# GpSimd relieved of sums and lo parts after attention, and a new order of the attention phase's pieces

## The chip, the cores and the metric

The kernel runs on one core of a Trainium2 chip. The core has five engines that run side by side, each through its own queue in order: TensorE (PE, matrix products into PSUM), VectorE (DVE), ScalarE (ACT), GpSimd (POOL) and SyncE (SP, which here issues nearly all DMAs). The metric is the device time of one execution in microseconds (us), the median of some runs.

## The reference, cut to what matters

```
q, k, v: (batch 2, 8 heads, 768, 64) float32
k_sum = max over blocks of 32 keys;  v_sum = mean over the same blocks        (24 summaries a head)
scores = concat(windowed q.kT / 8 with |i-j| < 16,  q.k_sumT / 8 + log 32);  a = softmax(scores)
x  = a @ concat(v, v_sum)              -> (1536 tokens, 512)
x  = relu(x @ w_in)**2 @ w_out         first layer, d_ff 2048
y  = gelu_sigmoid(x @ w_in2) @ w_out2  second layer, d_ff 2048    (float32; the kernel's weights arrive as 64-bit words)
```

## The kernel before, in words

**Precision.** A product of float32 operands is made of three single-pass products: each operand is split into a hi part (rounded) and a lo part (the rest), and PE adds hi·hi, hi·lo and lo·hi. `parts` (from L906) makes the two: the hi part by ACT (L913) or DVE (L914), the lo part, a subtraction of two operands in SBUF, by DVE or GpSimd (L918). `add` (from L892) makes sums and differences of two SBUF tiles on DVE or GpSimd (L902). Weights arrive as 512 KB `raw` tiles (L871 for w_in, L875 for w_out); ACT scales the upper words (L880), DVE puts the number together (L884, L887), and `parts` splits it. Some are saved to DRAM for a second use (L853) and fetched again (L857).

**Work.** The attention phase handles 12 tiles of 128 tokens. For a unit of 256 tokens, q and k are loaded and turned by PE: with `packed` 0 or 1 by four transposes for each half (L557), with `packed` 2 by eight products of 64 columns for each half (L561), whose load moves rows of 512 bytes in two DMAs of 256 KB (L411) instead of rows of 256 bytes (L418, `packed` 0). The first 768 keys come by another way (L432, L439, turned at L603). The summaries of v come from PE (L533, L507) out of three v loads of 512 KB each. `scores` (PE L692, DVE L707), `softmax` (ACT L722, DVE and GpSimd L726, L736, L729) and `tail` (PE L759 and L771, ACT L325) follow for each tile; a tail writes the tile's columns of `xh` and `xl`, the operands of the first layer. The first layer for tokens 0 to 511 runs among these pieces, block f of d_ff after block: `step` (PE L953 into `h`) and `finish` (PE L1008 into `acc`). Its first four blocks run in halves of 256 tokens (matmuls of 256 columns).

After attention the rest is matrix work. `layer` runs the second layer on tokens 0 to 511 (L953, L1010). `twice` runs each layer for the other 1024 tokens with fewer products: seven instead of eight for a 2x2 block matrix (L1395), once for w_in and, for 6 or 8 pairs of blocks, once more for w_out (`second`, L1300 in the first layer, L1302 in the second). The price is sums and differences of tiles (L902, `add`) and sums of a PSUM bank with an SBUF tile (L1309). In the second layer's `twice`, each of the eight pairs of blocks goes round one loop: products into three banks, sums out of them, the activation (ACT L1162), the differences t1 and t2 and their split into `gh` and `gl` (L902, L913, L918), and a `second` with them, for which PE waits; at the same time the next pair's weights are combined (four differences on half tiles of 128x256, twice: w_in for the next pair, w_out for this one).

**What sets the order.** `ORDER` lists the attention phase's pieces: `K`/`B` loads of k, `T` their turning, `q`, `k` loads of a unit (second number: the packing), `V` the v summaries, `w,f,z` a weight block (z 0: w_in, 1: w_out), `g` or `h` scores and softmax, `t` a tail, `s,f,half` and `S,f` a step. A planner goes through this list and then through the code after it. It puts each operation at the first gap of its engine at which its inputs are ready by its own table of costs, and at the end everything is emitted in the order of planned starts. So the place of a piece in `ORDER` says who asks first for an engine, not where the piece ends up, and each engine runs its list in order, waiting where the plan was wrong. The queue of SP is such a list too: a load whose buffer isn't free holds up all loads behind it.

For operations that two engines can do, `soonest` takes the one that ends first by the plan. GpSimd's choices carry `port=True`: the planner lets GpSimd and DVE's operations of that kind take turns on one shared line. After the attention phase, GpSimd's planned times are stretched by 1.25 (`SLACK`), and DVE gets a handicap (`LEAN`). `ALONE` is read in `soonest`, after attention alone:

```
if eng == "POOL" and port and self.alone:
    continue
```

In the planned gaps of PE up to the first use of bank acc3, short matmuls of the identity (`warm`, L1728) are put that compute nothing.

Of the kernel before, what the change touches and what calls it, by code (L numbers as in the profile page):

```python
# [22 lines left out]
CHAIN = "b2cp4p56"  # L23
EARLY = 1
AHEAD = (0, 1, 2)
ALONE = False
SLACK = 0.05, 1.25
LEAN = 1.5, 0.25
MIX = (2, 3, 4, 5)
# [4 lines left out]


ORDER = """
    m,1 sel K,1 m,2 B,1 m,0 w,0,0 K,0 B,0 T,0 T,1 q,0,2 T,2 T,3 tq,0 q,1,1 g,1,0 g,1,1 tq,1 selw V,0 V,1 V,2
    v,0 h,2,0 v,1 g,0,1 q,2,2 q,3,0 k,3,0 ps,0 t,1 h,3,0 h,2,1 g,0,0 tq,2 v,2 t,0 h,3,1 w,3,0 t,2 v,3 h,5,0
    tq,3 w,0,1 s,0,0 t,3 w,3,1 h,4,0 k,5,0 s,3,0 w,2,0 s,0,1 w,2,1 s,2,0 s,2,1 k,4,1 q,4,1 tk,3 v,4 w,1,0
    h,5,1 h,4,1 v,5 v,6 w,1,1 tk,4 tk,5 s,3,1 t,4 pk,3 w,6,0 t,5 h,6,0 w,7,0 s,1,0 sv,1 w,6,1 s,1,1 pk,4  # L40
    w,7,1 h,7,0 S,7 tq,4 w,4,0 w,4,1 h,7,1 S,6 w,11,0 w,11,1 pk,5 h,9,0 q,5,0 S,4 w,9,0 h,6,1 v,7 S,11 v,8
    ps,1 w,8,0 t,7 h,9,1 w,9,1 tq,5 w,10,0 w,10,1 S,9 v,9 w,15,0 t,6 w,8,1 t,9 S,8 w,5,0 S,10 w,12,0 h,10,0
    w,5,1 w,14,0 h,10,1 S,5 v,10 h,11,0 w,12,1 w,14,1 S,12 w,13,0 h,11,1 h,8,0 S,14 t,10 v,11 w,15,1 S,15
    h,8,1 t,11 w,13,1 S,13 t,8
"""


# [222 lines left out]
def kernel(  # L270
# [1428 lines left out]
    plan.lean = LEAN  # L1699
    plan.alone = ALONE  # L1700
    plan.slack = SLACK
# [60 lines left out]
```

## Time and profile before

| | us |
|---|---|
| median of 3 runs (lowest, highest) | 573.71 (573.65, 575.44) |
| the profiled execution, its own time | 576.52 |
| its span, first to last instruction | 574.8 |
| PE busy (share of the span) | 560.5 (98%) |
| DVE busy | 495.4 (86%) |
| ACT busy | 409.2 (71%) |
| GpSimd busy | 87.7 (15%) |

PE's busy time is a union of modelled, pipelined matmuls: that it is near 100% says that PE nearly always had a matmul under way, and a matmul of 512 columns starts every 0.23 us in a stretch without waits. The chain that ended last runs through PE for 79% of the span, through DVE for 10% and through DMAs for 6%.

### The profile page before, as it was taken

How to read it: one execution, taken by the hardware profiler on the slowest of the kernel's cores; microseconds unless marked ns; L12 is line 12 of the kernel's file. 1: busy time of each engine (PE TensorE's matmuls, PEld its weight loads, DVE VectorE, ACT ScalarE, POOL GpSimd, SP SyncE). 2: the span in 40 equal slices, each digit the busy share in tenths (PEclk: the TensorE clock that was granted, in tenths of full speed). 3: DMA queues.
4: the chain of work that ended last, by engine and by line, in shares of the span. 5: the costliest groups of instructions: out<-in, count | busy, mean ns of one | idle time of the engine just before them, and what ended most of it. 6: DMA issues, size and time to landing. Idle time of an engine off the chain costs nothing.

```text
span 574.8 us, 10960 instructions
## 1 busy us (share of the span) xinstructions
PE 560.5 (98%) x3766; PEld 476.8 (83%) x3766; DVE 495.4 (86%) x1072; ACT 409.2 (71%) x892; POOL 87.7 (15%) x153
## 2 busy tenths in 40 slices
PE   9899999999999999999999999999999999999997
PEld 8678888877878887888887888888778888899997
DVE  4788888989789999988998998989988888889983
ACT  5998889878886678787788856666456555687660
POOL 6323321012100000000020101001131233200200
PEclk9999999999999999999999999999999999999999
DMA  9999998897678765544668758574355554587653
GB/s 267 235 245 244 291 279 261 258 291 221 192 230 263 243 210 178 169 148 164 202 203 259 217 155 267 164 237 148 135 177 178 159 177 147 180 268 240 203 154 110
DMA packets 106711, 120.25 MB, mean 209 GB/s; under 512 B 32832, under 2 KB 74560, under 8 KB 106656
## 3 DMA queue, kind: packets, MB, share of 16 engines
q1 hardware_dynamic: 106464, 119.17, 68.4%
q8 instruction: 29, 0.48, 0.4%
q0 software_dynamic: 192, 0.39, 0.2%
q14 instruction: 26, 0.21, 0.1%
HBM read 86.64 MB, written 32.51 MB: 207 GB/s over the span
## 4 chain that ended last, share of the span: by engine, by line
PE 79%; DVE 10%; DMA 6%; ACT 2%; issue 1%; SPq 1%; POOL 0%; POOLq 0%; DVEq 0%
PE acc L1395 11%; PE m L1395 9%; PE acc L1302 8%; PE h L953 8%; PE acc L1008 7%; PE acc L1300 7%; PE m L1300 5%; PE m L1302 4%; PE acc L953 4%; PE m L1010 3%; PE acc L1010 2%; DMA raw<-in_moe_w_in_dram 2%; PE h L1302 2%; PE h L1300 2%; PE m L771 2%; PE m L953 1%
## 5 line engine op out<-in xcount | busy, mean ns | idle before, releaser
L918 DVE TENSOR_TENSOR w<-xw,w 128x512 fp32r<-128x512 f32 (+1 forms) x138 | 83.7, 621 | 4.5 <-ACT w L913 3.5
L913 ACT CAST w<-xw 128x512 fp32r<-128x512 f32 (+1 forms) x132 | 70.5, 552 | 21.8 <-DVE xw L887 14.9
L953 PE MATMUL h<-xh,w 128*128 128x512 f32 (+1 forms) x184 | 55.7, 365 | 1.3 <-DVE w L918 0.7
L880 ACT ACTIVATE raw<-raw 128x512 f32<-128x512 f32 x72 | 48.1, 680 | 8.4 <-DMA raw<-in_moe_w_out_dram 6.2
L1395 PE MATMUL m<-top,w 128*128 128x512 f32 x210 | 53.5, 392 | 0.6 <-ACT w L325 0.6
L887 DVE SCALAR_TENSOR_TENSOR xw<-raw,xw 128x512 uint32<-128x512 uint32 x68 | 46.7, 688 | 3.9 <-ACT raw L880 1.7
L1395 PEld LDWEIGHTS m<-top,w 128*128 128x128 f32 x210 | 38.6, 188 | 8.9 <-ACT w L325 1.4
L1395 PE MATMUL acc<-top,w 128*128 128x512 f32 x174 | 44.5, 391 | 0.0
L1008 PE MATMUL acc<-gh,w 128*128 128x512 f32 (+1 forms) x160 | 42.2, 350 | 0.1
L1395 PE MATMUL acc<-xh,w 128*128 128x512 f32 x124 | 41.8, 389 | 0.0
L953 PEld LDWEIGHTS h<-xh,w 128*128 128x128 f32 x184 | 33.1, 188 | 8.0 <-DVE w L918 1.0
L884 DVE TENSOR_SCALAR xw<-raw 128x512 uint32<-128x512 uint32 x68 | 29.1, 429 | 11.6 <-DMA raw<-in_moe_w_in_dram 9.3
L1395 PEld LDWEIGHTS acc<-top,w 128*128 128x128 f32 x174 | 32.2, 188 | 7.3 <-ACT w L325 0.4
L722 ACT ACTIVATE sm<-sm,st 128x120 f32<-128x120 f32 x96 | 36.6, 385 | 0.2
L913 ACT CAST top<-gs 128x512 fp32r<-128x512 f32 x40 | 24.7, 619 | 13.6 <-DVE gs L902 5.1
L953 PE MATMUL h<-xl,w 128*128 128x512 f32 (+1 forms) x92 | 32.8, 356 | 0.3 <-DVE xl L784 0.3
L1008 PEld LDWEIGHTS acc<-gh,w 128*128 128x128 f32 x160 | 27.8, 189 | 4.3 <-issue 0.5
L918 DVE TENSOR_TENSOR top<-gs,top 128x512 fp32r<-128x512 f32 x38 | 27.0, 713 | 3.0 <-ACT top L913 2.5
L1302 PE MATMUL acc<-w,gh 128*128 128x256 f32 x136 | 28.2, 283 | 0.0
L1008 PE MATMUL acc<-gl,w 128*128 128x512 f32 (+1 forms) x80 | 27.9, 349 | 0.0
L1395 PEld LDWEIGHTS acc<-xh,w 128*128 128x128 f32 x124 | 23.3, 188 | 4.9
L918 DVE TENSOR_TENSOR w<-w,w 128x256 fp32r<-128x256 f32 (+1 forms) x48 | 24.8, 522 | 1.6 <-ACT w L913 1.4
(301 smaller groups left out, 1532.1 us busy)
## 6 DMA issues: line engine op xcount, KB each, us to landing
raw<-in_moe_w_in_dram SPq DMA_DIRECT2D x36, 512.0 KB, 4.9
raw<-in_moe_w_out_dram SPq DMA_DIRECT2D x36, 512.0 KB, 4.5
w<-xw SPq DMA_DIRECT2D x52, 256.0 KB, 2.5
xw<-w SPq DMA_DIRECT2D x29, 256.0 KB, 2.8
w<-w SPq DMA_DIRECT2D x23, 256.0 KB, 2.8
g<-r SPq DMA_DIRECT2D x16, 256.0 KB, 2.1
r<-g SPq DMA_DIRECT2D x16, 256.0 KB, 3.2
vw<-in_v_dram SPq DMA_DIRECT2D x20, 192.0 KB, 6.2
```

What stands on the lines that cost most here:

```text
L722: nc.scalar.activation(out=s.t[:, h, :], in_=s.t[:, h, :], func=AF.Exp, bias=st.t[:, 0, h:h + 1], scale=-1.0, accum_out=st.t[:, 1, h:h + 1])
L880: nc.scalar.activation(out=top, in_=top, func=AF.Prelu, scale=-(2.0 ** -80), alpha=-(2.0 ** -32))
L884: op("DVE", 0.36, lambda: nc.vector.tensor_scalar(out=x.t, in0=raw.t[:, :, 0], scalar1=29, scalar2=None, op0=ALU.logical_shift_right), rea ...
L887: op("DVE", 0.64, lambda: nc.vector.scalar_tensor_tensor(out=x.t, in0=raw.t[:, :, 1], scalar=3, in1=x.t, op0=ALU.logical_shift_left, op1=A ...
L913: plan.soonest([("ACT", 0.09 + 0.44 * fr, False, lambda: nc.scalar.copy(out=hi.t[:, hc], in_=src())), ("DVE", 0.05 + 0.4 * fr, True, lambd ...
L918: eng.tensor_tensor(out=lo.t[:, lc], in0=src(), in1=hi.t[:, hc].bitcast(F32), op=ALU.subtract)
L953: nc.tensor.matmul(hp.t[:, cols], lhsT=w.t[:, kc * P:(kc + 1) * P], rhs=x.t[:, kc, cols], start=(kc == 0 and n == 0), stop=(kc == KC - 1 a ...
L1008: nc.tensor.matmul(a.t[:, cols], lhsT=w.t[:, j * P:(j + 1) * P], rhs=g.t[:, cols], **st)
L1010: nc.tensor.matmul(a.t, lhsT=g.t[:, j * P:(j + 1) * P], rhs=w.t, **st)
L1300: nc.tensor.matmul(b.t, lhsT=w.t[:, x + j * P:x + j * P + P], rhs=g.t, **st)
L1302: nc.tensor.matmul(b.t[:, (j % 2) * CH:(j % 2) * CH + CH], lhsT=g.t[:, j * P:j * P + P], rhs=w.t[:, x:x + CH], **st)
L1395: nc.tensor.matmul(bank.t, lhsT=a, rhs=rhs(b, kh), start=(begin and k == 0 and n == 0), stop=(k == 1 and n == 2), skip_group_check=True)
```

## The change

Two things are changed, both numbers and no code. `ALONE` becomes True: in the code after the attention phase, GpSimd is no longer offered sums (`add`, `whole`), lo parts (`parts`, and the `gl` of `step`). What reads PSUM was never offered to it. And `ORDER` is another list: the same 16 weight blocks, 12 tiles and 6 units, in another order, with other packings of some loads (q1, k3, k4 now 2, before 1, 0, 1; q2 now 0, before 2; q3 and k5 now 1, before 0), and with other weight blocks first.

```
-ALONE = False
+ALONE = True
 ...
-    m,1 sel K,1 m,2 B,1 m,0 w,0,0 K,0 B,0 T,0 T,1 q,0,2 T,2 T,3 tq,0 q,1,1 g,1,0 g,1,1 tq,1 selw V,0 V,1 V,2
 ...
+    B,0 selw w,3,0 m,2 m,0 K,0 T,0 T,1 K,1 B,1 T,3 q,0,2 T,2 tq,0 w,1,0 w,0,0 g,1,0 q,1,2 sel tq,1 m,1 g,0,1
 ...
```

**SP's queue at the start of the program.** `kin` holds k and later v, `qin` q, `raw` a weight block, `vw` the windows of v. Before:

```order
L432 DMA kin_103<-in_k_dram 128x4x256
L439 DMA kin_108<-in_k_dram 128x4x128
L871 DMA raw_116<-in_moe_w_in_dram 128x4x256
L432 DMA kin_137<-in_k_dram 128x4x256
L439 DMA kin_108<-in_k_dram 128x4x128
L411 DMA qin_182<-in_q_dram 128x4x128 x2
L411 DMA qin_212<-in_q_dram 128x8x128
L432 DMA kin_244<-in_v_dram 128x4x256
L432 DMA kin_266<-in_v_dram 128x4x256
L439 DMA kin_290<-in_v_dram 128x8x128
```

and in the changed kernel:

```order
L439 DMA kin_87<-in_k_dram 128x4x128
L871 DMA raw_97<-in_moe_w_in_dram 128x4x256
L432 DMA kin_119<-in_k_dram 128x4x256
L432 DMA kin_147<-in_k_dram 128x4x256
L439 DMA kin_87<-in_k_dram 128x4x128
L411 DMA qin_165<-in_q_dram 128x4x128 x2
L871 DMA raw_208<-in_moe_w_in_dram 128x4x256
L871 DMA raw_231<-in_moe_w_in_dram 128x4x256
L411 DMA qin_255<-in_q_dram 128x4x128 x2
L432 DMA kin_288<-in_v_dram 128x4x256
L432 DMA kin_310<-in_v_dram 128x4x256
L439 DMA kin_333<-in_v_dram 128x8x128
```

Three weight blocks (blocks 3, 1 and 0) now stand ahead of the three v loads, where one stood.

**DVE in the second layer's `twice`, one turn of the loop** (t1 and t2 are the first two differences of 128x512, `xw` and `part` combined weights of w_in and w_out). Before:

```order
L902 TENSOR_TENSOR xw_5651<-w_5607 128x256
L902 TENSOR_TENSOR xw_5653<-w_5574,w_5607 128x256
L902 TENSOR_TENSOR r_5662<-gs_2710,w_5546 128x512
L902 TENSOR_TENSOR r_5667<-gs_2771,r_5662 128x512
L902 TENSOR_TENSOR gs_2710<-gs_2771,gs_2710 128x512
L918 TENSOR_TENSOR gl_5683<-r_5662,gh_5669 128x512
L918 TENSOR_TENSOR gl_5687<-r_5667,gh_5675 128x512
L1309 TENSOR_TENSOR w_5692<-acc_5647,r_5655 128x512
L918 TENSOR_TENSOR w_5640<-w_5607,w_5640 128x256
```

and in the changed kernel:

```order
L902 TENSOR_TENSOR r_5679<-gs_2756,w_5565 128x512
L902 TENSOR_TENSOR r_5684<-gs_2817,r_5679 128x512
L902 TENSOR_TENSOR gs_2756<-gs_2817,gs_2756 128x512
L918 TENSOR_TENSOR gl_5700<-r_5679,gh_5686 128x512
L918 TENSOR_TENSOR gl_5704<-r_5684,gh_5692 128x512
L1309 TENSOR_TENSOR w_5709<-m_5666,r_5672 128x512
L902 TENSOR_TENSOR xw_5717<-w_5618 128x256
L902 TENSOR_TENSOR xw_5723<-w_5603,w_5618 128x256
L902 TENSOR_TENSOR xw_5717<-xw_5717,w_5603 128x256
L902 TENSOR_TENSOR xw_5723<-w_5603,xw_5717 128x256
```

The four differences of w_in, of which DVE did two ahead of t1 and GpSimd two beside t1 and t2, now all stand on DVE behind `gl`. The order of PE's instructions in this loop (36 of L1395, 12 of L1302, 6 of L1395, 12 of L1302) is the same in both.

## Rows read from the trace of the kernel before

**Rows 1.** Busy time in stretches: start:end, length, each engine's busy us (instructions), PEclk, DMA, GB/s.
```profile
0.00:25.00 25.00, 21.81 (x346) 18.94 (x348) 13.74 (x62) 16.64 (x53) 11.50 (x56) 1.00 0.98 255
25.00:50.00 25.00, 23.39 (x340) 20.90 (x336) 21.90 (x91) 22.22 (x79) 6.88 (x14) 1.00 1.09 252
50.00:75.00 25.00, 23.25 (x289) 21.08 (x287) 20.62 (x54) 22.03 (x65) 10.26 (x22) 1.00 1.02 259
...
275.00:300.00 25.00, 25.00 (x111) 20.58 (x110) 23.86 (x47) 19.89 (x37) 3.22 (x3) 1.00 0.61 196
...
163.00:575.00 412.00, 404.01 (x2080) 343.88 (x2078) 362.87 (x656) 273.84 (x510) 46.28 (x43) 1.00 0.60 192
```

**Rows 2.** What PE waited for, whole span: total us, times, longest.
```profile
PE m L1302 <- DVE gl L918: 3.4, 5, 1.2
PE m L533 <- DMA kin<-in_v_dram: 1.5, 2, 1.2
...
PE h L953 <- DVE w L918: 0.7, 1, 0.7
PE m L1395 <- ACT w L325: 0.6, 1, 0.6
```

**Rows 3.** Timeline of a turn with GpSimd beside DVE: start, duration, engine, instruction, [idle before].
```profile
444.95 0.69 DVE L1309 TENSOR_TENSOR gs<-m,r 128x512 f32<-128x512 f32 x1 [1.09 <-PE m L1395]
446.71 0.80 POOL L902 TENSOR_TENSOR xw<-xw,w 128x256 f32<-128x256 f32 x1 [4.79 <-DVE xw L902]
446.83 1.22 DVE L902 TENSOR_TENSOR r<-gs,w 128x512 f32<-128x512 f32 x1
...
448.61 1.19 POOL L902 TENSOR_TENSOR part<-xw 128x256 f32<-128x256 f32 x1
...
450.19 0.28 PE L1302 MATMUL m<-w,gh 128*128 128x256 f32 x1
450.27 1.28 DVE L918 TENSOR_TENSOR gl<-r,gh 128x512 fp32r<-128x512 f32 x2
451.00 0.39 PE L1302 MATMUL m<-w,gl 128*128 128x256 f32 x1 [0.54 <-DVE gl L918]
...
463.42 0.28 PE L1302 MATMUL m<-w,gh 128*128 128x256 f32 x1
```

**Rows 4.** Timeline of the turn before it, without GpSimd in these operations.
```profile
435.62 0.69 DVE L902 TENSOR_TENSOR gs<-gs,gs 128x512 f32<-128x512 f32 x1
436.23 1.29 DVE L918 TENSOR_TENSOR gl<-w,gh 128x512 fp32r<-128x512 f32 x2
...
437.75 0.28 PE L1302 MATMUL m<-w,gh 128*128 128x256 f32 x1
...
438.03 0.41 DVE L902 TENSOR_TENSOR xw<-xw,w 128x256 f32<-128x256 f32 x1
```

**Rows 5.** Groups by shape, DVE, from 163 us on: count | busy us, mean ns.
```profile
L902 DVE TENSOR_TENSOR gs<-gs,gs 128x512 f32<-128x512 f32 x30 | 23.7, 791 | 0.1
```

**Rows 6.** The chain that ended last, in the attention phase: start, us, what.
```profile
12.28 7.08 DMA kin<-in_v_dram
...
28.37 7.04 DMA raw<-in_moe_w_in_dram
...
54.38 7.01 DMA raw<-in_moe_w_out_dram
```

**Rows 7.** Timeline of PE in the attention phase.
```profile
11.61 1.92 PE L561 MATMUL m<-ident,qin 128*64 128x128 f32 x32
...
37.64 0.39 PE L953 MATMUL h<-xh,w 128*128 128x256 f32 x1 [0.55 <-ACT xh L325]
...
57.91 1.04 PE L557 MATMUL m<-ident,kin 128*128 128x128 f32 x8
58.70 0.36 PE L953 MATMUL h<-xh,w 128*128 128x256 f32 x1
```

**Rows 8.** PE's groups by line from 0 to 75 us: the matmuls that compute nothing.
```profile
L1728 PE MATMUL warm<-ident 128*128 128x128 f32 x34 | 6.8, 354 | 1.4 <-POOL ident masks.py:199 1.4
```

More of the change, by code (lines that the diff above doesn't have):

```diff
@@ L36 @@
 ORDER = """
-    m,1 sel K,1 m,2 B,1 m,0 w,0,0 K,0 B,0 T,0 T,1 q,0,2 T,2 T,3 tq,0 q,1,1 g,1,0 g,1,1 tq,1 selw V,0 V,1 V,2
[L38 to L44, printed above, removed]
+    B,0 selw w,3,0 m,2 m,0 K,0 T,0 T,1 K,1 B,1 T,3 q,0,2 T,2 tq,0 w,1,0 w,0,0 g,1,0 q,1,2 sel tq,1 m,1 g,0,1
+    g,1,1 V,0 V,1 V,2 v,0 g,0,0 v,1 v,2 ps,0 t,1 h,3,0 k,3,2 t,0 h,2,0 w,1,1 h,2,1 k,4,2 v,3 h,3,1 s,1,0
+    tk,3 t,3 w,0,1 q,2,0 tk,4 t,2 s,0,0 w,3,1 tq,2 w,2,0 h,4,0 w,2,1 s,3,0 k,5,1 s,0,1 s,3,1 s,2,0 q,3,1
+    s,2,1 q,5,0 s,1,1 tq,3 w,9,0 w,4,0 tk,5 h,5,0 pk,3 w,7,0 w,7,1 w,4,1 w,6,0 S,4 h,7,0 tq,5 S,7 v,4 pk,5
+    h,4,1 w,9,1 t,4 S,9 w,5,0 w,8,0 sv,1 h,6,0 v,5 pk,4 h,5,1 h,7,1 w,8,1 v,6 w,11,0 S,8 t,5 q,4,1 w,11,1
+    w,6,1 S,6 tq,4 S,11 h,9,0 w,5,1 w,12,0 S,5 w,10,0 ps,1 h,6,1 v,7 t,7 h,11,0 w,10,1 w,15,0 S,10 w,12,1
+    w,13,0 v,8 v,9 t,6 h,8,0 S,12 v,10 h,11,1 v,11 w,14,0 h,9,1 t,9 t,11 h,8,1 h,10,0 w,15,1 w,13,1 w,14,1
+    S,15 t,8 S,14 h,10,1 S,13 t,10
 """
```

## Prediction

> **What bounds the kernel now.** I read the busy time by stretches first, then what PE waited for, then the timeline of the stretches in which it waited, last the chain of waits. From 75 us on PE is full nearly everywhere: 25.00 of 25 us in a stretch such as 275 to 300 [rows 1]. So nothing that only shifts work on DVE, ACT or GpSimd there counts, unless PE waits for it. PE loses time in three places. At the start, in 75 us, it is idle for 3.19 + 1.61 + 1.75 = 6.55 us [rows 1], and 34 matmuls of 6.8 us compute nothing [rows 8]; part of that is the wait for the first load, which no order can take away. In the second layer's `twice` it waits five times, 3.4 us in all, for a lo part `gl` of DVE, and once 0.6 us for ACT just ahead of that loop [rows 2]. The rest is the end of the program. So the change has two halves that hardly touch: `ALONE` acts on the five waits, `ORDER` on the first 75 us.
>
> **ALONE: the five waits.** After 163 us GpSimd does 43 operations in 46.28 us [rows 1], 33 of them of 128x256 and 10 of 128x512. In a turn of the loop with GpSimd, its differences run from 446.71 to 449.80; beside them DVE's difference of 128x512 takes 1.22 us, the next ones as long, and `gl` is ready so late that PE, which came at 450.19, goes on at 451.00 [rows 3]. In the turn before, without GpSimd in this place, the same difference takes 0.69 us, the step from one such operation to the next is 0.61 us, and PE doesn't wait [rows 4]. In the changed order seven operations of 128x512 lead from the sum L1309 to the first `gl`: 7 x 0.61 = 4.3 us after 444.95 is 449.2, a microsecond before PE comes. GpSimd's differences now stand on DVE behind `gl`; their users come a third of a turn later. So the wait should go in all five turns. What it is worth: 3.4 us by the waits; by the turns, 463.42 - 450.19 = 13.23 us with a wait [rows 3] against 450.19 - 437.75 = 12.44 without [rows 3, 4], 0.8 us four times and about 1.5 for the first, longest one, 4.7 us. The low end is 1.5 us, if half of the waits come back as waits for the weights combined later. I take 3.8, nearest to the waits themselves with a part of the 0.6 us.
>
> **ALONE: what DVE gets for it.** By 0.41 us for 128x256 [rows 4] and 0.69 for 128x512 [rows 4], the 43 operations are 33 x 0.41 + 10 x 0.69 = 20.4 us at most, against 412 - 362.87 = 49 us in which DVE is free [rows 1]. It saves what the sharing costs now: at least 30 x (0.79 - 0.69) = 3 us, in the one group of differences that shows it best [rows 5], at most half of GpSimd's 46 us, 23. In the loop that matters it is 3 x 0.53 = 1.6 us saved [rows 3, 4] for three operations of 0.41 = 1.2 us added, so a turn gets no longer. In 275 to 300 us DVE is busy 23.86 of 25 us and takes over three operations, 0.41 + 0.41 + 0.69 = 1.5 us, for 3.22 us of GpSimd [rows 1]: with a third of that saved it stays just under 25. I cost this at nothing; its cover is the buffers between DVE and PE, and without cover a lag of 1 us or so could reach PE.
>
> The Trainium skill, GPSIMD Engine Reference, section Key points, says that GpSimd shares its SBUF interfaces with VectorE, which contends when VectorE's instruction has two SBUF inputs. By that rule the doubling seen in rows 3 goes with GpSimd's work, as I have it. Were the 1.22 us due to something else, a turn would gain 1.2 us of DVE work and save none; that case stands below as a rival.
>
> **ORDER: work added to PE.** Of the units that go through the eight-matmul turning (`packed` 2), there are four instead of two. One costs PE 1.92 us, a unit with transposes 58.70 - 57.91 = 0.79 us, to the start of the next matmul [rows 7]. That is 2 x 1.13 = +2.3 us. It costs nothing as far as PE would have idled there.
>
> **ORDER: the loads.** The chain at the start goes through DMAs: the third v load, 12.28 to 19.36; block 3's w_in, issued only at 28.37, 7.04 us; a w_out that lands at 54.38 + 7.01 = 61.4 us [rows 6]. The DMA engines are full all that time (share 0.98 to 1.09) at about 255 GB/s [rows 1], so what is loaded earlier pushes something back. The new queue takes two more weight blocks, 1.05 MB, ahead of v: 1.05 / 0.255 = 4.1 us, so the v summaries' last load lands at about 23.5 instead of 19.4 us. PE's summary of v stands in its queue ahead of most scores and the first tails, so PE waits there; it has 1.13 us more to do before, with the q unit turned the dear way. Price: 0 to 4.1 - 1.1 = 3 us. ACT and DVE meanwhile split the weights and can do the scores that were issued before; I take 1 us. In return the first half blocks have their w_in by some 16 us, and the first L953, at 37.64 us [rows 7], needn't share its moment with the splitting of a weight that landed at 35.4; the last w_out of the half blocks, now at 61.4, comes earlier too. PE can win what it loses between 25 and 75 us: 3.4 us idle [rows 1] and up to half of the 6.8 us of empty matmuls [rows 8], 0 to 6 us. I take half, 3 us. The start: +2.3 + 1 - 3 = +0.3, between -2.7 (6 won, 1 lost, 2.3 added) and +5.3 or, with nothing hidden at all, 4.1 + 2.3 = +6.4.
>
> **Sum.** -3.8 + 0.3 = -3.5 us. The profiled execution took 576.52 us, its span 574.8 and 1.7 around it, and would take 573.0. It lies 2.8 us above the median of the runs, 573.71; the same difference from there gives 570.2 us.
>
> **Rivals.**
> - *The start pays for the loop.* The weights' gain is eaten by the wait for v (3 and 3), and the dearer turnings stay: +2.3 - 3.8 = -1.5, 572.2 us; with a little less in the loop 572.7, no change that can be told. For it: the DMA engines are full [rows 1], and an order that takes one thing sooner takes another later. Against it: PE idles in the first 25 us anyway [rows 1].
> - *v comes too late.* The 4.1 us lie on the path whole, as the chain runs from the v load on [rows 6], the weights win nothing because ACT is then held by the softmax and by weights that land in its queue's way, and 2.3 us of turnings come on top: +6.4 - 3.8 = +2.6, 576.3 us, slower. It decides where the first L953 starts later than 37.64 + 4.1, about 42 us. Against it: work that was waiting for weights can follow without a gap.
> - *DVE becomes the bound.* If the sharing isn't what made DVE slow, GpSimd's 43 operations come on top, turns get 1.2 us more on DVE, and the waits stay: +0.3 + 0, 574.0 us. Against it: the two turns of rows 3 and 4 differ in nothing else.
> - *The start wins in full.* -2.7 - 3.8 = -6.5, 567.2 us. For it: three w_in blocks early, when ACT and DVE are least busy (16.64 and 13.74 of 25 us) [rows 1].
>
> **How the numbers follow.** About 1.7 us, 0.3%, is what a measurement here tells from no change: faster is below 572.0, slower above 575.4. Forecast 0.48 (its own range 568.3 to 572.0, -5.4 to -1.7 us), the start in full 0.13: faster 0.61. The start pays 0.19 and DVE the bound 0.09: the same 0.28. v too late 0.11: slower. The predicted time is 570.2. For 8 in 10 the range goes from 566.8, a little above where the full win ends (-2.7 - 4.7 is 566.3), to 574.6, and leaves out the slower case.
>
> **What would show it.** In the changed profile: no sums and lo parts of GpSimd after the attention phase; in the second layer's `twice` all differences of 128x512 at 0.6 to 0.7 us, no wait of L1302 for `gl`, turns of 12.4 to 12.7 us; DVE busier by a few us at most from 163 us on. At the start: the v wait of L533 grows from 1.5 to some 3 to 5 us, the first L953 at 34 to 38 us, fewer waits behind it, and PE's idle time in 75 us not above 7 us. The prediction is wrong in its first half if PE still waits at L1302, or at L1395 for weights instead; in its second half if the busy time of PE to 75 us changes by more than 3 us beyond the 2.3 us that are added.

## The result, and the profile after

The changed kernel takes 569.66 us (median of 4 runs, 569.16 to 570.43), the kernel before 574.14 on the same chip (4 runs): ratio 0.9913, 95% interval 0.9898 to 0.9928, so 4.1 to 5.9 us faster; the medians lie 4.5 us apart. The prediction was 570.2. The profiled execution took 569.57 us, its span 567.9.

Busy time in the stretches of [rows 1] (start:end, length, then PE, PEld, DVE, ACT, POOL; PEld is TensorE's loading of weights; granted clock, DMA share, GB/s):

```profile
0.00:25.00 25.00, 21.61 (x302) 19.39 (x303) 14.96 (x54) 15.71 (x48) 9.90 (x53) 0.93 0.95 263
25.00:50.00 25.00, 24.39 (x389) 21.50 (x389) 22.29 (x72) 23.23 (x77) 11.15 (x24) 1.00 1.08 267
50.00:75.00 25.00, 25.00 (x243) 23.71 (x242) 20.54 (x66) 22.53 (x61) 8.74 (x14) 1.00 0.98 281
275.00:300.00 25.00, 25.00 (x111) 20.33 (x110) 24.24 (x49) 20.18 (x37) 0.00 (x0) 1.00 0.63 207
163.00:568.00 405.00, 401.10 (x2075) 343.13 (x2073) 366.09 (x702) 273.52 (x503) 0.00 (x0) 1.00 0.60 195
```

GpSimd (POOL) is gone after attention: 0.00 us, where it had 46.28 [rows 1]. DVE has only 3.2 us more from 163 us on. In the first 75 us PE's idle time is 3.39 + 0.61 + 0 = 4.00 us instead of 6.55.

What PE waited for, in the whole span (total us, times, longest), against [rows 2]:

```profile
PE m L561 <- DMA qin<-in_q_dram: 1.9, 1, 1.9
PE warm L1728 <- POOL band L353: 1.4, 1, 1.4
PE acc L1302 <- DVE r L1617: 0.5, 1, 0.5
PE acc L771 <- ACT pT L325: 0.5, 2, 0.3
```

The five waits for `gl` have no successor in this list. The waits for v (L533) are gone from it too, and one for the load of q1 stands in their place.

The same place in a turn of the second layer's `twice` as in [rows 3], timeline of DVE and PE:

```profile
443.02 0.68 DVE L902 TENSOR_TENSOR r<-gs,w 128x512 f32<-128x512 f32 x1
443.73 0.69 DVE L902 TENSOR_TENSOR r<-gs,r 128x512 f32<-128x512 f32 x1
444.34 0.69 DVE L902 TENSOR_TENSOR gs<-gs,gs 128x512 f32<-128x512 f32 x1
444.94 1.29 DVE L918 TENSOR_TENSOR gl<-r,gh 128x512 fp32r<-128x512 f32 x2
446.45 0.28 PE L1302 MATMUL m<-w,gh 128*128 128x256 f32 x1
446.56 0.28 PE L1302 MATMUL m<-w,gl 128*128 128x256 f32 x1
```

All three differences are back at 0.69 us. The first `gl` ends at 444.94 + 0.69 = 445.63, so 0.82 us before PE comes to L1302, and the matmul with `gl` follows the one with `gh` after 0.11 us. The next turn's first L1302 starts at 458.89: a turn of 12.44 us.

How large the wait was before is best read where TensorE's weight load waits (`gl` is the stationary operand here). Weight loads of the kernel before:

```profile
PEld m L1302 <- DVE gl L918: 4.9, 5, 1.5
```

The same five waits have 3.4 us in PE's own list [rows 2]. There the modelled end of the matmul before hides the first part: between 450.19 and 451.00 [rows 3] stand 0.81 us, in PE's row 0.54. The turns said 4.7.

### The profile page after: what moved, and what is told of

It is laid out like the page before. It is cut to its first block, busy times and chain, and to the rows that moved or that the text cites. A ratio compares the mean times of both kernels' runs of the same rounds, so it can differ in the third digit from the quotient of the medians.

```text
span 567.9 us, 10985 instructions
## 1 busy us (share of the span) xinstructions
PE 560.1 (99%) x3816; PEld 479.7 (84%) x3816; DVE 499.8 (88%) x1117; ACT 411.6 (72%) x892; POOL 42.4 (7%) x112
## 4 chain that ended last, share of the span: by engine, by line
PE 91%; ACT 4%; SPq 1%; DMA 1%; DVE 1%; issue 0%; ACTq 0%
PE acc L1395 17%; PE m L1395 10%; PE h L953 9%; PE acc L1008 8%; PE acc L1302 7%; PE acc L1300 6%; PE m L1300 6%; PE m L1302 5%; PE acc L1010 4%; PE acc L953 4%; PE m L1010 3%; PE m L953 2%; ACT sm L722 2%; PE h L1302 2%; PE h L1300 2%; PE m L771 2%
## 5 line engine op out<-in xcount | busy, mean ns | idle before, releaser
L918 DVE TENSOR_TENSOR w<-xw,w 128x512 fp32r<-128x512 f32 (+1 forms) x142 | 85.2, 612 | 2.9 <-ACT w L913 1.9
L913 ACT CAST w<-xw 128x512 fp32r<-128x512 f32 (+1 forms) x125 | 66.9, 550 | 20.4 <-DVE xw L887 13.6
L1395 PE MATMUL acc<-top,w 128*128 128x512 f32 x246 | 62.2, 391 | 0.0
L953 PE MATMUL h<-xh,w 128*128 128x512 f32 (+1 forms) x184 | 55.6, 364 | 0.0
L1395 PEld LDWEIGHTS acc<-top,w 128*128 128x128 f32 x246 | 45.5, 188 | 9.4 <-ACT r L325 0.4
L1395 PE MATMUL acc<-xh,w 128*128 128x512 f32 x116 | 39.5, 389 | 0.0
L953 PEld LDWEIGHTS h<-xh,w 128*128 128x128 f32 x184 | 33.1, 189 | 5.6 <-issue 1.0
L1395 PE MATMUL m<-top,w 128*128 128x512 f32 x138 | 35.7, 393 | 0.0
L953 PE MATMUL h<-xl,w 128*128 128x512 f32 (+1 forms) x92 | 32.5, 353 | 0.0
L918 DVE TENSOR_TENSOR top<-gs,top 128x512 fp32r<-128x512 f32 x42 | 28.7, 688 | 2.5 <-ACT top L913 2.0
L1395 PEld LDWEIGHTS m<-top,w 128*128 128x128 f32 x138 | 25.4, 188 | 6.2 <-ACT w L325 0.8
L1395 PE MATMUL m<-xh,w 128*128 128x512 f32 x76 | 26.3, 389 | 0.0
L1395 PEld LDWEIGHTS acc<-xh,w 128*128 128x128 f32 x116 | 21.8, 188 | 4.6
```

The costliest lines, as they stand in the source:

```text
L913: plan.soonest([("ACT", 0.09 + 0.44 * fr, False, lambda: nc.scalar.copy(out=hi.t[:, hc], in_=src())), ("DVE", 0.05 + 0.4 * fr, True, lambd ...
L918: eng.tensor_tensor(out=lo.t[:, lc], in0=src(), in1=hi.t[:, hc].bitcast(F32), op=ALU.subtract)
L953: nc.tensor.matmul(hp.t[:, cols], lhsT=w.t[:, kc * P:(kc + 1) * P], rhs=x.t[:, kc, cols], start=(kc == 0 and n == 0), stop=(kc == KC - 1 a ...
L1395: nc.tensor.matmul(bank.t, lhsT=a, rhs=rhs(b, kh), start=(begin and k == 0 and n == 0), stop=(k == 1 and n == 2), skip_group_check=True)
```

## The experiments

Each time is a median, beside the kernel before on the same chip (574.02 us for the first four, 574.08 for the next three, then 575.18 and 574.69); ratios are to that.

**The two halves alone.** The order before, with GpSimd taken out after attention:

```
-ALONE = False
+ALONE = True
```

> The old order of the attention phase, ALONE True: the first half of the change by itself. Theory: the gain comes from the five waits of PE for gl in the second layer's loop, 3.4 us by the waits and 4.7 by the length of turns, so 3.3 to 4.5 us less than before, no wait of L1302 for gl, turns of 12.4 to 12.7 us, and the start as before (PE idle about 6.5 us in 75 us). Rival (the new order carries the change): 0 to 1.5 us less than before. Rival (DVE becomes the bound): no change or slower, waits for gl still there.

Measured 569.72 us, ratio 0.9926 (0.991 to 0.9942): all of the gain. No wait for `gl`, and turns of 12.44 us.

The new `ORDER` with `ALONE = False`:

> The new order, ALONE False: the second half by itself. Theory: PE's idle time in 75 us falls by 2.5 us as in the changed kernel and 2.3 us of turnings are added, so 0 to 1.5 us less than before, and five or so waits of L1302 for gl of 3 to 4 us remain. Rival (the order carries the change): 3 to 4.5 us less than before. Rival (the two halves need each other): slower than before or far from the sum.

Measured 575.14 us (12 runs), ratio 1.0013 (0.9999 to 1.0027): nothing, or up to 1.6 us lost. What PE waited for:

```profile
PE m L1302 <- DVE gl L918: 3.4, 5, 1.2
PE m L561 <- DMA qin<-in_q_dram: 1.4, 2, 1.0
PE m L533 <- DMA kin<-in_v_dram: 1.2, 1, 1.2
PE acc L603 <- DMA kin<-in_k_dram: 0.8, 1, 0.8
```

The five waits for `gl`, 3.4 us, are there as before.

**Where in the program.** `ALONE` only for the second layer's `twice` (and what follows):

```
+        plan.alone = True
         twice(1, 2, 1, two)
```

> The old order, GpSimd left out of the second layer's twice alone; before that it does its sums and lo parts as in the kernel before. Theory: the loop is where GpSimd costs time, so nearly all of what ALONE brings is here, 3 to 4 us less than before. Rival (the sharing costs DVE and so PE everywhere after attention): less than half of what ALONE brings by itself.

Measured 569.47 us, ratio 0.9922 (0.9905 to 0.9939): that loop is the whole gain, as far as these times can tell. The opposite, `ALONE` everywhere after attention but there:

```
+        plan.alone = False
         twice(1, 2, 1, two)
```

> The old order, GpSimd left out of all that follows attention up to the second layer's twice, and used in that as before. Theory: PE has no waits there that GpSimd makes, so within 1 us of before, and the five waits for gl stay. Rival (sharing costs everywhere): more than half of what ALONE brings by itself, 2 us or more.

Measured 569.96 us, ratio 0.9935 (0.9914 to 0.9955). This expectation was wrong: the gain is there, and no wait for `gl`, although GpSimd does 16 operations of 15.28 us between 400 and 500 us. Timeline of a turn, GpSimd and DVE:

```profile
443.53 0.69 DVE L902 TENSOR_TENSOR r<-gs,r 128x512 f32<-128x512 f32 x1
443.67 1.16 POOL L902 TENSOR_TENSOR part<-xw 128x256 f32<-128x256 f32 x1 [3.51 <-DVE r L902]
444.14 1.23 DVE L902 TENSOR_TENSOR gs<-gs,gs 128x512 f32<-128x512 f32 x1
445.30 1.28 DVE L918 TENSOR_TENSOR gl<-r,gh 128x512 fp32r<-128x512 f32 x2
```

The planner, starting from another state, gave GpSimd one operation beside this chain instead of three. That one stretches one difference, 1.23 for 0.69 us, and `gl` comes 0.54 us later. PE has 0.8 us to spare, so it doesn't wait. A new theory: sharing makes DVE slow as predicted, but there is a margin of about 0.8 us, and only what exceeds it is paid.

**The sharing by itself.** The order before with `ALONE = True`, and GpSimd subtractions of 128x256 on a scratch tile that compute nothing. DVE and TensorE keep their lists, so the turn differs in nothing else. (In these kernels L1415 is L1395.)

```
+                    nc.gpsimd.tensor_tensor(out=d, in0=d, in1=y, op=ALU.subtract)
 ...
+            op("POOL", 1.2, go, after=list(x.writer.values()))
 ...
+            if m:
+                beside(t1, ("", "2", "22", "222", "2222", "1111", "2000")[n] if n < 7 else "")
             add(t2, ALL, gs[f1], ALL, t1, ALL, sub=True)
```

> The order before with ALONE True, and in the second layer's twice extra GpSimd operations on a scratch tile of 128x256 that compute nothing, let go when t1 is done, so that they lie beside t2, the third difference and the two gl: none in the first turn, then 1, 2, 3 and 4 subtractions (two operands in SBUF), then 4 copies (one operand), then a subtraction and 3 memsets. VectorE's and TensorE's lists are unchanged. Theory (sharing with a margin): with ALONE True the first gl is ready about 0.8 us before TensorE comes to L1302 and is read some 0.25 us later, so a margin of 1.05 us; a VectorE operation of 128x512 with a GpSimd subtraction beside it takes 1.22 instead of 0.69 us, so the turn with 1 and the turn with 2 wait for nothing or under 0.1 us (0.5 and 1.0 us late), the turns with 3 and 4 wait about 0.5 us each. Rival (GpSimd's work as such, or a queue that is merely too long, makes the wait): either all turns with GpSimd in them wait, or none. Of the copies and memsets neither theory knows a price: 0.69 to 1.22 us for the operation beside them.

One execution, 569.58 us, of which only the turns are read. Of those with one subtraction, four, four copies, and a subtraction with three memsets, the third difference and the `gl` behind it, and what lay beside:

```profile
430.53 1.18 POOL L1324 TENSOR_TENSOR idle<-idle,r 128x256 f32<-128x256 f32 x1 [279.78 <-DVE r L902]
431.02 1.23 DVE L902 TENSOR_TENSOR gs<-gs,gs 128x512 f32<-128x512 f32 x1
432.17 0.68 DVE L918 TENSOR_TENSOR gl<-r,gh 128x512 fp32r<-128x512 f32 x1
...
468.91 1.22 DVE L902 TENSOR_TENSOR gs<-gs,gs 128x512 f32<-128x512 f32 x1
469.66 2.98 POOL L1324 TENSOR_TENSOR idle<-idle 128x256 f32<-128x256 f32 x3
470.05 1.10 DVE L918 TENSOR_TENSOR gl<-r,gh 128x512 fp32r<-128x512 f32 x1
...
482.08 2.35 POOL L1326 COPY idle<-idle 128x256 f32<-128x256 f32 x3
482.49 0.88 DVE L918 TENSOR_TENSOR gl<-r,gh 128x512 fp32r<-128x512 f32 x1
...
494.93 1.06 POOL L1328 MEMSET idle<- 128x256 f32 x3
495.35 0.68 DVE L918 TENSOR_TENSOR gl<-part,gh 128x512 fp32r<-128x512 f32 x1
```

A subtraction beside it costs DVE's operation 0.4 to 0.5 us, a copy 0.2, a memset nothing. t2, which had started 0.12 us before GpSimd came (430.41), kept its 0.69 us, so the most that `gl` could be late is 0.54 + 0.42 = 0.96 us, not the 1.5 expected. The turns from one first L1302 to the next: 12.44 us with one subtraction (433.12 to 445.56), 12.63 with two, 12.83 with three, 12.76 with four, 12.44 with the copies. So neither all of these turns wait nor none, and the rival falls. One subtraction fits into the margin (0.54 us late), two no longer (0.19 us lost, where under 0.1 was expected). That puts the margin between 0.54 and 0.96 us, under the 1.05 of the expectation and in keeping with the 0.8 read above.

Four subtractions in seven turns, at the same place:

> The order before with ALONE True, and in each of seven turns of the second layer's twice four GpSimd subtractions of 128x256 on a scratch tile that compute nothing, let go when t1 is done, beside t2, the third difference and the two gl. VectorE has the same list as with ALONE True alone (569.7 us). Theory (sharing): the first gl comes 1.5 us later, of which 1.05 us are margin, so TensorE waits about 0.5 us in seven turns: waits of L1302 for gl of 2.5 to 4.5 us, time 572.0 to 574.0. Rival (the wait came from the two differences that VectorE had ahead of t1, not from the sharing): 569.7, no waits for gl.

Measured 572.20 us (10 runs), ratio 0.9969 (0.9957 to 0.9981): against 0.9926 without them 2.5 us are back. PE's own list shows one wait of 0.6 us, the list of the weight loads all seven:

```profile
PEld m L1302 <- DVE gl L918: 2.4, 7, 0.9
```

A turn is 472.12 - 459.31 = 12.81 us, 0.37 more than without; seven times that is 2.6; the first of the seven, 433.74 - 420.44 = 13.30, is longer. With DVE's list untouched, GpSimd's presence alone brings back more than half of the loss.

The same subtractions, let go only when the second `gl` is done:

```
+                if m and t is t2 and n + 1 < len(fs):
+                    beside(gl, "2222")
```

> As the kernel with four idle GpSimd subtractions a turn, but they are let go when the second gl is done, so that they lie beside the sum L1309 and the combined weights behind it. The same 28 subtractions. Theory (place decides): VectorE gets up to 2 us a turn more there, where the weights have a third of a turn to spare, so no wait for gl and 569.7 plus 0 to 1 us. Rival (any GpSimd work in the loop costs what it takes from VectorE, wherever it lies): like the other place, 572 to 574 us, with waits of TensorE at L1395 for w.

Measured 571.33 us, ratio 0.9955 (0.9937 to 0.9973), 1.7 us more than without, between the two theories. Timeline of DVE and GpSimd:

```profile
458.08 0.68 DVE L1309 TENSOR_TENSOR r<-m,w 128x512 f32<-128x512 f32 x1
458.31 0.74 POOL L1324 TENSOR_TENSOR idle<-idle,gl 128x256 f32<-128x256 f32 x1 [9.70 <-DVE gl L918]
459.25 0.83 DVE L902 TENSOR_TENSOR xw<-w,w 128x256 f32<-128x256 f32 x1
```

What TensorE's weight loads waited for from 400 to 530 us, two rows of it:

```profile
PEld acc L1415 <- ACT part L325: 0.4, 2, 0.2
PEld m L1415 <- ACT r L325: 0.4, 2, 0.2
```

No wait for `gl`, and for a combined weight only the 0.4 us that is there with `ALONE` alone too. But the combined weights come later (0.83 for 0.42 us), ACT's split of them too, and behind that in ACT's queue the copy out of a bank (L325), for which PE waits (with `ALONE` alone these two rows are not there). That this copy is late because it stands behind the split is argued from the order, not tried. The sum L1309, one operand of which is in PSUM, keeps its 0.68 us while a GpSimd subtraction lies beside it.

**The parts of ORDER.** Two edits of the changed kernel, and one of the order before with `ALONE = True`. Three packings as before:

```
-q,1,2  k,3,2  k,4,2
+q,1,1  k,3,0  k,4,1
```

> The changed kernel with the packings of three units as before (q1 1, k3 0, k4 1, where it has 2), its order otherwise kept. Theory (added turning is real work of TensorE where it has no gap): three units turned with transposes instead of eight matmuls a half, 3 x 1.13 = 3.4 us less; q1's lies ahead of the wait for v and saves little, k3 and k4 stand where TensorE is full: 569.7 less 2.3 gives 567.4, between 566.3 and 568.6. Rival (the packings serve the loads: rows half as long take longer, and the scores of these units come late): 569.7 to 571.5.

Measured 577.18 us, ratio 1.0039 (1.0027 to 1.0051): 7.2 us slower than the changed kernel, where 2.3 faster was expected. PE's idle time to 75 us goes from 4.00 to 75 - 65.63 = 9.37 us. Three of its waits:

```profile
PE m L557 <- ACT qT L325: 1.7, 1, 1.7
PE m L533 <- DMA kin<-in_v_dram: 1.3, 1, 1.3
PE h L953 <- DVE r L969: 0.9, 1, 0.9
```

Loads are in it too (q1 0.8 us, a k unit 0.7), so the rival, that the packings serve the loads, has something for it, though the loss is far larger than it said.

Two weight blocks behind the v loads:

```
-tq,0 w,1,0 w,0,0 g,1,0 q,1,2 sel tq,1 m,1 g,0,1 g,1,1 V,0 V,1 V,2 v,0
+tq,0 g,1,0 q,1,2 sel tq,1 m,1 g,0,1 g,1,1 V,0 V,1 V,2 w,1,0 w,0,0 v,0
```

> The changed kernel with its second and third weight block (blocks 1 and 0 of w_in) listed behind the three v loads instead of ahead of them. Theory (early weights are what the order wins): the wait for q1 of 1.9 us goes or shrinks, but the first half blocks come later, TensorE's idle time in 75 us grows from 4.0 towards the 6.55 us of before: 570.5 to 572.5. Rival (the place of these two loads decides nothing): 569.7 within 0.6.

Measured 572.25 us, ratio 0.995 (0.9938 to 0.9962), 2.1 us slower than the changed kernel. The wait for q1 is gone, the first L953 is at 37.6 us again and PE's idle time to 75 us 7.15, with one wait of 2.3 us for a softmax (L729). The profiled execution is the slowest of the six, 573.87 us: its granted clock is 0.50 from 25 to 30 us, behind that wait. The other five kept a mean clock of 0.999 or more, with a median of 572.21 us, so the loss isn't the clock's. In the order before, `q,2,2` made `q,2,0`:

> The order before with ALONE True, and unit q2 loaded with packing 0 (transposes) instead of 2. Theory (turning costs TensorE what it takes there): one unit of 1.13 us less, 568.6 if nothing hides it, 568.2 to 569.7. Rival (the start is set by loads and waits, the work is hidden): 569.6, within 0.5.

Measured 573.65 us (12 runs), ratio 0.998 (0.9967 to 0.9992): 3.1 us slower than without the edit, where 1.1 faster was expected, and outside the rival's range too. So taking dear turnings away cost time twice. I took it that they pay by their faster loads, as the DMA engines are full there, and tried the other direction. The new packings in the order before:

```
-q,1,1  k,3,0  k,4,1
+q,1,2  k,3,2  k,4,2
```

> The order before with ALONE True and the packings of the new order (q1 2 instead of 1, k3 2 instead of 0, k4 2 instead of 1), no other entry of the list changed. Theory (packing 2 pays for its 1.13 us of TensorE a unit with faster loads, since the DMA engines are full up to 75 us and rows of 256 bytes take their time): k3's rows of 256 bytes go, small packets to 75 us fall from 18,400 to about 16,400, and more MB land by 75 us; 569.6 less 0 to 2 us. Rival (added turning is a cost, and taking it away was harmful only because any edit of a searched list upsets it): 571 to 574, slower by the 3.4 us of turning or by the upset.

Measured 577.96 us, ratio 1.0062 (1.0039 to 1.0085), 7.8 us slower than without the edit, more than either side expected. The theory fails at its first step: the small packets to 75 us fall from 18,448 to 18,212 only, and 19.38 MB land by then instead of 19.91. And one more in the changed kernel, `q,2,0` made `q,2,2`:

> The changed kernel with unit q2 at packing 2 instead of 0, no other entry changed. Theory (packing 2 pays by faster loads): 2,000 small packets fewer to 75 us, 1.13 us of TensorE more, 569.7 within 1 us. Rival (any edit of the searched list upsets it): 571.5 or more, with new waits of TensorE up to 75 us.

Measured 572.15 us, ratio 0.9949 (0.9932 to 0.9965), 2.1 us slower, although the small packets to 75 us fall from 13,984 to 12,575. The rival was right here. All five edits, in either list and either direction, cost some 2 to 8 us. A difference of two such ratios is good to about 1 us; by the medians the two of 2.1 us are 1.6 and 1.9.

Where the two largest losses lie can be read from PE's busy time in the whole profile. First `ALONE` alone and the changed kernel, then each of them with the edit of three packings:

```profile
PE 556.9 (98%) x3766; PEld 476.1 (84%) x3766; DVE 500.1 (88%) x1120; ACT 411.6 (73%) x887; POOL 42.6 (8%) x110
PE 560.1 (99%) x3816; PEld 479.7 (84%) x3816; DVE 499.8 (88%) x1117; ACT 411.6 (72%) x892; POOL 42.4 (7%) x112
...
PE 563.0 (98%) x3840; PEld 480.3 (83%) x3840; DVE 501.6 (87%) x1118; ACT 409.3 (71%) x892; POOL 40.6 (7%) x109
PE 559.8 (97%) x3758; PEld 476.9 (83%) x3758; DVE 502.4 (87%) x1115; ACT 414.9 (72%) x892; POOL 44.2 (8%) x112
```

The spans are 567.0, 567.9, 575.8 and 575.2 us, so PE is idle for 10.1, 7.8, 12.8 and 15.4 (one execution each, and the ends of matmuls are modelled). Where three dear turnings are added, most of the loss is work: 6.1 us more busy, of which the rows of the turnings (L557 and L561) make 3.0 (15.0 us instead of 12.0), and 2.7 more idle; the granted clock is 0.93 from 25 to 50 us there. Where three are taken away, all of the loss is waiting: 7.6 us more idle. The turnings' rows do fall, from 15.1 to 11.5, but 50 instead of 36 empty matmuls (L1728) fill up gaps. So the turnings' work is there in both cases, and an edit of the list moves other waits by more than that. In three of the five (k3's, k4's and q1's packings in both lists, and q2 at packing 0) PE even waits 0.9 us for ACT after the attention phase, where neither unedited kernel has such a wait. The price of a single entry cannot be read by editing it, and which displacement costs what stays open. That each list holds together because it was tuned as a whole is a guess that fits; no run tests it.

## Why the prediction was right, and where it was not

**The five waits: right, and a little larger.** Predicted 3.8 us (1.5 to 4.7). Measured with the order untouched: 0.0074 x 574 = 4.2 us with `ALONE` everywhere, 4.5 with it in the last loop. The weight loads' 4.9 us and the 4.7 of the turns were nearer than PE's own list, which hides the start of each wait; I had kept close to that list. Turns of 12.44 us and differences of 0.69 are as foretold.

**The cause: right, with a threshold that the prediction lacked.** It said that GpSimd's work nearly doubles DVE's differences beside it. The idle subtractions show it with nothing else changed. They refute the rival "DVE becomes the bound", by which the sharing isn't what made DVE slow. The Trainium skill, GPSIMD Engine Reference, section Key points, has the contention where VectorE's instruction has two SBUF inputs; the trace agrees, 1.10 to 1.23 us for such an operation and 0.68 still for the sum L1309, which reads one operand from PSUM. Against that rival I had written that the two turns of rows 3 and 4 differ in nothing else. That was wrong: in rows 3 DVE also does two differences of 128x256 ahead of t1. It did no harm to the sum. The turn of rows 3 from the sum L1309 on, then the same place with `ALONE` alone:

```profile
446.15 0.42 DVE L902 TENSOR_TENSOR xw<-w 128x256 f32<-128x256 f32 x1
446.49 0.42 DVE L902 TENSOR_TENSOR xw<-w,w 128x256 f32<-128x256 f32 x1
...
440.39 0.69 DVE L1309 TENSOR_TENSOR gs<-acc,r 128x512 f32<-128x512 f32 x1 [1.74 <-PE acc L1395]
444.14 1.29 DVE L918 TENSOR_TENSOR gl<-r,gh 128x512 fp32r<-128x512 f32 x2
```

From L1309 to the start of `gl` the turn of rows 3 takes 450.27 - 444.95 = 5.32 us, with `ALONE` alone 444.14 - 440.39 = 3.75. Of these 1.57 us, the three stretched differences make 1.5; the two differences ahead (0.68) are set off by a lo part of 0.60 that now stands there. What the prediction lacked is the threshold. It had `gl` ready about a microsecond early, but didn't use that as a margin: one stretched difference costs nothing, as the kernel with `ALONE` everywhere but in this loop shows.

**DVE's added work at nothing: right.** 3.2 us more after attention, and 24.24 of 25 us at 275 to 300, as the prediction had it (just under 25).

**The start: its sum right, its terms in part.** Predicted +0.3 us (-2.7 to +6.4), measured +0.7 (-0.1 to +1.6) for the order alone, and no difference from the order before on top of `ALONE` (0.9913 and 0.9926, their intervals overlap). The third v summary in the order before and with the new order alone:

```profile
19.41 0.64 PE L533 MATMUL m<-kin,band 128*24 128x128 f32 x16 [1.17 <-DMA kin<-in_v_dram]
22.09 0.64 PE L533 MATMUL m<-kin,band 128*24 128x128 f32 x16 [1.18 <-DMA kin<-in_v_dram]
```

- *The wait for v.* It comes 2.7 us later; I had v at 23.5 us. The wait for it is 1.2 us, not 3 to 5: TensorE comes later itself, since the load of q1 stands behind the same two weight blocks and makes it wait 1.4 us there. I had counted these blocks against v only. That the two waits together grow by about the 1 us that I took for v (1.4 + 1.2, against 1.5 before) was luck. In the profile of the changed kernel q1's wait is 1.9 us and v's is gone.
- *The early weights.* The first L953 at 34.59 us and 4.00 us of idle time lie in the ranges given, and putting the two blocks back costs about 2 us, against the 3 that I took. Yet making q2's turning dearer costs as much, so this is no clean price.
- *The turnings, +2.3 us.* As work of PE they are there: the rows of L557 and L561 make 12.0 us in the order before and 14.3 with the new order alone. In the changed kernel they make 15.1, of which 1.0 is a low clock that I hadn't foreseen (last section). The two profiles with `ALONE` True, one execution each, show both sides of the sum: with the new order PE is busy for 3.2 us more, about what the turnings' rows gain, and idle for 2.3 less, where I had 3 won and 1 lost. As the price of single entries I can't confirm it: taking three such turnings away costs 7.2 us, adding three to the other list 7.8, far from 3.4 either way. The two edits that I expected to be faster by this price were slower.

No version that was run can be told to be faster than `ALONE` alone; the new order, then, bought nothing that these times show.

## What to carry to other kernels

When an engine off the critical path slows the one that feeds TensorE, don't count its work: find the chain that it lies beside, add up how much each link is stretched, and subtract the margin with which the result arrives; here up to 0.5 us a link against 0.8. Read waits of TensorE from the weight loads as well as the matmuls. And where a planner places everything anew behind each edit, a new order can be checked by its two totals, PE's work and PE's waiting, but not by taking single entries back: predict it as a whole, with a range that says so.

## What the runs showed of the hardware that was not expected

A wait sometimes cost TensorE its clock, and sometimes not. The changed kernel and the one with q2's packing 2 are idle at the same place for q1 (1.94 and 2.45 us). Rows of windows around that wait (start:end, length, PE's busy us, granted clock, DMA share, GB/s), and q1's turning behind it, first in the changed kernel, then in the other:

```profile
14.00:16.50 2.50, 0.72 (x20) 1.00 1.12 361
17.70:20.70 3.00, 3.00 (x42) 0.50 1.18 274
...
16.66 2.96 PE L561 MATMUL m<-ident,qin 128*64 128x128 f32 x32 [1.94 <-DMA qin<-in_q_dram]
```

```profile
14.00:16.50 2.50, 0.30 (x12) 1.00 1.09 349
17.70:20.70 3.00, 3.00 (x72) 1.00 1.23 281
...
16.76 1.97 PE L561 MATMUL m<-ident,qin 128*64 128x128 f32 x32 [2.45 <-DMA qin<-in_q_dram]
```

At 0.50, the lower of the two levels (1.2 GHz), the 32 matmuls of q1's turning take 2.96 us instead of 1.97. In the changed kernel this cost little that shows: its third v summary ends at 23.34 us without a wait, in the other kernel, at the full clock but with a wait for v of 1.48 us, at 23.67. The kernel alone doesn't decide it: over four executions of the changed kernel the mean granted clock is 0.996, 1.000, 0.998 and 0.997.

And the price of sharing depends on GpSimd's operation: beside a subtraction DVE's lo part of 128x512 takes 1.10 us, beside a copy 0.88, beside a memset 0.68, as if alone.
